# At most two attention steps behind one FFN step from block 2 on, and q of tile 5 loaded ahead of V of tile 4

## Chip, cores and metric

The kernel runs on one core of one Trainium2 chip. The metric is the device time of one execution in microseconds (us): the median of 5 runs of the kernel before is 341.76 us (341.69 to 342.01).

## What is computed

Causal attention with a sliding window of 128 keys and a bias that falls linearly with distance (8 batches, 8 heads, 576 positions, head size 64), and a gated feed-forward block (FFN) on its output, 4608 tokens of 512 wide:

```python
scores = scale * q @ k.T + slopes * (-abs(rel))        # only where 0 <= rel < 128
attn = exp(scores - max) / sum
x = (attn @ v).transpose(0, 2, 1, 3).reshape(4608, 512)
g = x @ w_gate                                         # 512 x 1536
out = (g * sigmoid(g) * (x @ w_val)) @ w_out           # 1536 x 512
```

## The kernel before

**Attention** works on 36 units, nine for each pair of batches (`units`): eight tiles of 128 queries, and one unit that joins the two leftover half tiles. For unit i, `scores(i)` (line 244) takes products of k and q on TensorE (line 280) into four PSUM banks, four exponentials on ScalarE (line 286), and two products with a mask on VectorE (line 292). `weighted(i)` (line 328) multiplies the exponentials with V on TensorE (`av`, line 348) in two halves of four heads, each into a bank of its own, and divides by the sums on VectorE (lines 350 and 351). `x_transposed(i)` brings the result into the layout that the FFN reads (`xT`).

**The FFN** works on nine blocks of 512 tokens. For each of 12 slices of the inner width, `gate_val` (line 432) makes two groups of four matmuls (line 400): `pg` with the gate weights, after which ScalarE makes a tanh (`tt`, line 418) and VectorE a product (`uu`, line 419), and `pv` with the value weights, after which VectorE makes `hT` (line 430). The output products are made for the block before, in between (line 454 for block 0; line 535, with sums of tiles S from lines 488 to 491, for the later ones). Blocks 6 to 8 use another scheme for the first products (line 624), when attention is over.

**PSUM.** The banks of `scores`, of `av` and of some others come from one pool of four buffers in turn (`ps_a`, tag a). A bank is taken again when its reader is done. `pg` and `pv` come from another pool of three (`ps_f`, tag gv).

**The order.** Both parts are generators. `attention()` (line 851) yields after each attention step: the products and the first exponential of `scores` are a step each, the second exponential with the first mask product is one, and so on; from unit 13 on (`LATE`), `weighted(i)` stands inside of `scores(i + 1)`, as a step after the third. `ffn()` yields after each FFN step, with the amount of work (1.0 for a `pg` or a `pv` group, 0.75 for an output product). `everything()` (line 950) takes one FFN step, and then attention steps until their number `n_att` reaches a target that grows with the FFN's work (lines 976 to 984), or until enough tiles are done for the block that comes next (`ready`):

```python
            else:
                target = 84 + (step - 57) * RATE / 34.5
            while (n_att < target or done < ready[blk]) and att_step():
                pass
```

From step 60 on, the last step of block 1, the program's order is binding for TensorE alone (lines 965 to 967). On ScalarE and VectorE a scheduler sets the order when the kernel is built; in the trace each engine starts its instructions in that order.

**Loads.** GpSimd issues the loads of k, q, V and the weights, in an order written out by hand for the first eleven tiles (lines 892 to 925). Each load signals one of eight completion semaphores, in turn, and a load is issued only when the load eight places before it, on the same semaphore, has landed. Tiles 4 to 10 of k and q are transposed on TensorE (line 218), tiles from 11 on by a DMA that SyncE issues (line 239).

Of the kernel before, what the change touches and what calls it, by code (L numbers as in the profile page):

```python
# [51 lines left out]
def kernel(  # L52
# [54 lines left out]
    def later_masks(n, many):  # L107
        for h in by_slot[n:n + many]:
            nc.scalar.activation(reg[:, slot(h), :], dist, AF.Exp, scale=-(2.0 ** (-8.0 * (h + 1) / H)))
# [15 lines left out]
    def make_masks():  # L125
        nc.scalar.copy(msk[0][:, :, 0:64], reg[:, :, 128:192])
        nc.scalar.copy(msk[1][:, :, 64:128], reg[:, :, 128:192])
        nc.scalar.copy(msk[2][0:64, :, 0:64], reg[0:64, :, 0:64])
        nc.scalar.copy(msk[2][64:128, :, 64:128], reg[64:128, :, 64:128])
# [18 lines left out]
    def busy(n):  # L148

        t_ = ps_f.tile([P, 512], FP32, name="nil", tag="po", bufs=1)  # L150
        for _ in range(n):
            nc.tensor.matmul(t_, idle[:, 0:P], idle, start=True, stop=True)
# [20 lines left out]
    def source(src, rank):  # L173

        s, c = divmod(rank, 9)
        if c == 8:
            return [((64 * n, 64 * n + 64),
                     src[2 * s + n, :, 512:576, :].rearrange("h p d -> p h d")) for n in range(2)]
        b, t = 2 * s + c // 4, c % 4
        return [((0, P), src[b, :, t * P:(t + 1) * P, :].rearrange("h p d -> p h d"))]  # L180

    def load_v(rank):
        va[rank] = va_all[rank % NV]
        for (p0, p1), src in source(v, rank):
            nc.gpsimd.dma_start(va[rank][p0:p1, :, 0:D], src)  # L185

    def load_qk(rank, which="kq"):
        for name in which:
            t_ = nat.tile([P, H, D], FP16, name=name + "n", tag=name + "n")
            for (p0, p1), src in source(k if name == "k" else q, rank):  # L190
                nc.gpsimd.dma_start(t_[p0:p1], src)  # L191
            (natk if name == "k" else natq)[rank] = t_

    def load(rank):
        load_qk(rank)
        load_v(rank)
# [626 lines left out]
    def first_tiles():  # L823

        first_masks()
        transposes_to(need[0] + 1)
        for n, _ in enumerate(run(scores(0))):
            if n == 0:
                transposes_to(need[1])
        for i in range(FIRST):  # L830
            if i + 1 < FIRST:
                for n, _ in enumerate(run(scores(i + 1))):
                    if n == 0 and i + 2 < FIRST:
                        transposes_to(need[i + 2])
            weighted(i)

            if i >= 2:
                begin(4, i - 1)
            if i > 0:
                x_transposed(i - 1)  # L840
        begin(6, 2)
        begin(4, 3)
        gate(0, 0, early[(0, 0, "g")][0], 0, 384)
        x_transposed(FIRST - 1)
        val(0, 0, early[(0, 0, "v")][0], 0, 384)
        later_masks(0, 2)
        gate(0, 1, early[(0, 1, "g")][0], 0, 384)
        val(0, 1, early[(0, 1, "v")][0], 0, 384)
        begin(6, 3)
# [35 lines left out]
    def load_w(c0, c1):  # L885
        for src, dst in ((wg2, wg_sb), (wv2, wv_sb)):
            nc.gpsimd.dma_start(dst[:, :, c0:c1], src[:, :, c0:c1])
# [13 lines left out]
    load_w(0, 256)  # L901
    load_w(256, 512)
    load_w(512, 768)
    load(4)
    load_qk(5, "q")
    load_w(768, 1024)
    load_qk(5, "k")
    load_qk(6)
# [18 lines left out]
    done = n_att = 0  # L927
    ready = [4, 8, 13, 17, 22, 26, 31, 35, 36]

    def att_step():  # L930
        nonlocal done, n_att
        r = next(att, None)
        if r is not None:
            done = r
            n_att += 1
        return r is not None
# [7 lines left out]
    def progress(steps):  # L944
        total = 0.0
        for size in steps:
            total += size
            yield total

    def everything():  # L950
        nonlocal done
        base = 0
        busy(WARM)
        with tc.manual_schedule(engines=ENGINES[MANUAL]):
            first_tiles()
            done = FIRST
            steps = progress(ffn())
            while (at := next(steps)) < ALONE:
                if at == 2.0:
                    nc.scalar.copy(idm2, idm)  # L960
                if at in (1.0, 3.0, 4.0):
                    later_masks(2 * (1, 3, 4).index(at) + 2, 2)
        fixed = ExitStack()
        for step in steps:
            if step >= FIXED_FROM and fixed is not None:
                fixed.enter_context(tc.manual_schedule(engines=ENGINES["pe"]))
                fixed, held = None, fixed
            if step == MASKS_AT:
                make_masks()

            b1 = 24 + 3 * PRE

            lead = LEAD if done < X_DMA_FROM - 2 else LEAD + 4
            blk = (0 if step + LEAD < b1 else 1 if step + LEAD < 60
                   else min(NBLK - 1, 2 + int((step + lead - 60) // 34.5)))
            if step < b1:

                target = base + 1.25 * max(0, step - ALONE) + 1.5 * max(0, step - 16)
            elif step < 60:
                target = base + 32 + SECOND * 8 * (step - b1) / (60 - b1)  # L980
            else:
                target = 84 + (step - 57) * RATE / 34.5
            while (n_att < target or done < ready[blk]) and att_step():
                pass
        held.close()

    everything()
    queue.close()

# [29 lines left out]
```

## Time and profile before

| what | value |
|---|---|
| median of 5 runs | 341.76 us (341.69 to 342.01) |
| the profiled execution's own time | 341.76 us |
| its span, first to last instruction | 340.0 us, so 1.76 us lie around it |
| granted TensorE clock, mean | 0.996 |
| busy share of the span: TensorE, VectorE, ScalarE, GpSimd | 97%, 81%, 61%, 32% |
| chain of work that ended last | TensorE 72%, VectorE 18%, ScalarE 5% |

In the views, PE is TensorE's matmuls, PEld its weight loads, DVE VectorE, ACT ScalarE, POOL GpSimd. A row of the timeline gives the start, the length of the merged run of instructions, engine, line, output and inputs, and in brackets the idle time of the engine just before, with what ended it. Matmul ends are modelled and reach past the start of the next one, so lengths of neighbours overlap; the distance between starts is what the engine spends.

### The profile page before, as it was taken

The page shows a single profiled execution, that of the slowest core. Times are in us where ns is not written, and L with a number is a line of the kernel's source. Part 1 is how long each engine was busy: PE and PEld are TensorE (multiplying, and loading weights), DVE is VectorE, ACT ScalarE, POOL GpSimd, SP SyncE. Part 2 cuts the span into 40 slices and gives each one's busy share as a digit, 9 for nine tenths or more (in the row PEclk, how much of TensorE's full clock was granted, in tenths as well). Part 3 has the DMA queues.
Part 4 walks back from the last instruction along what each step waited for, and adds up shares of the span by engine and source line. Part 5 has one row for each costly group of instructions (what it writes and reads, how often), then busy time and mean ns, then how long its engine had stood idle before and what let it go on. Part 6 is the DMA issues. An engine that isn't in the chain of part 4 may idle for free.

```text
span 340.0 us, 7782 instructions
## 1 busy us (share of the span) xinstructions
PE 329.9 (97%) x2983; PEld 219.2 (64%) x2983; DVE 276.6 (81%) x651; ACT 207.3 (61%) x413; POOL 109.6 (32%) x136
## 2 busy tenths in 40 slices
PE   7999999999999999999999999999999999999994
PEld 4484445444455665566665655666688888888883
DVE  5577985999888779998899999999865885775682
ACT  3758676565675676666665647563467776776650
POOL 8968682548765267644008000000000000000000
PEclk9999999999999999999999999999999999999998
DMA  9999999899999999999979903031101101011014
GB/s 150 167 180 177 166 164 161 75 134 153 153 168 155 157 175 176 158 161 146 191 139 104 177 19 94 15 61 49 64 2 62 52 12 65 2 63 64 0 64 124
DMA packets 160037, 37.37 MB, mean 110 GB/s; under 512 B 147328, under 2 KB 155648, under 8 KB 160000
## 3 DMA queue, kind: packets, MB, share of 16 engines
q0 software_dynamic: 118336, 18.62, 82.3%
q1 hardware_dynamic: 40976, 17.64, 28.1%
q10 hardware_dynamic: 688, 0.62, 0.6%
q8 instruction: 23, 0.38, 0.5%
q14 instruction: 14, 0.11, 0.1%
HBM read 37.91 MB, written 9.44 MB: 139 GB/s over the span
## 4 chain that ended last, share of the span: by engine, by line
PE 72%; DVE 18%; ACT 5%; issue 3%; DVEq 0%; ACTq 0%
PE po L535 15%; PE pg L400 12%; PE pv L400 11%; PE gX L624 9%; PE gY L624 5%; DVE hT L430 4%; PE av L348 4%; DVE uu L419 3%; PE ps L280 3%; PE p L535 3%; PE gZ L624 2%; DVE x L351 2%; DVE ex L292 2%; PE po L454 2%; ACT tt L418 2%
## 5 line engine op out<-in xcount | busy, mean ns | idle before, releaser
L400 PE MATMUL pv<-xT,wv_sb 128*128 128x512 f16 (+2 forms) x320 | 76.5, 358 | 0.6 <-DVE uu L419 0.2
L400 PE MATMUL pg<-xT,wg_sb 128*128 128x512 f16 (+2 forms) x320 | 75.8, 358 | 0.3 <-DVE xT L376 0.2
L418 ACT ACTIVATE tt<-pg 128x512 f16<-128x512 f32 (+2 forms) x70 | 41.3, 590 | 47.9 <-PE pg L400 47.0
L286 ACT ACTIVATE ex<-ps 128x512 f16<-128x512 f32 x96 | 50.0, 605 | 10.1 <-PE ps L280 10.1
L419 DVE SCALAR_TENSOR_TENSOR uu<-tt,pg 128x512 f16<-128x512 f16 (+2 forms) x69 | 46.0, 667 | 10.6 <-ACT tt L418 10.5
L430 DVE TENSOR_TENSOR hT<-uu,pv 128x512 f16<-128x512 f16 (+2 forms) x70 | 46.7, 667 | 3.0 <-PE pv L400 1.3
L185 POOL DMA_DIRECT2D va<-in_v_dram x40 | 34.2, 864 | 36.2 <-PE av L348 28.3
L400 PEld LDWEIGHTS <-wv_sb 128*128 128x128 f16 x320 | 28.3, 98 | 25.1 <-issue 3.2
L535 PEld LDWEIGHTS <-hT 128*128 128x128 f16 x384 | 37.2, 98 | 10.7 <-issue 0.8
L400 PEld LDWEIGHTS <-wg_sb 128*128 128x128 f16 x320 | 28.2, 98 | 23.3 <-issue 2.2
L191 POOL DMA_DIRECT2D kn<-in_k_dram x39 | 33.3, 858 | 18.1 <-DMA kT<-kn 11.5
L191 POOL DMA_DIRECT2D qn<-in_q_dram x39 | 33.4, 861 | 17.9 <-DMA va<-in_v_dram 10.8
L535 PEld LDWEIGHTS <-S 128*128 128x128 f16 x288 | 27.4, 98 | 7.2 <-issue 1.4
L292 DVE TENSOR_TENSOR ex<-ex,m_reg 128x1024 f16<-128x1024 f16 x42 | 28.8, 687 | 2.9 <-ACT ex L286 2.8
L351 DVE TENSOR_TENSOR x<-av,rec 128x256 f16<-128x256 f32 x72 | 28.8, 420 | 0.4
L535 PE MATMUL po<-T,S 128*128 128x256 f16 x192 | 25.9, 273 | 0.3 <-ACT u2s L561 0.3
L535 PE MATMUL po<-T,hT 128*128 128x256 f16 x192 | 26.0, 272 | 0.1
L320 ACT ACTIVATE exc<-psc 128x512 f16<-128x512 f32 x40 | 21.3, 607 | 1.9 <-PE psc L316 1.9
L678 DVE TENSOR_TENSOR hT<-s,v 128x512 f16<-128x512 f16 x18 | 7.6, 424 | 17.7 <-ACT s L677 17.7
L348 PEld LDWEIGHTS <-ex 128*128 128x128 f16 x384 | 17.4, 97 | 4.6 <-issue 1.3
L348 PE MATMUL av<-va,ex 128*128 128x65 f16 x384 | 19.3, 193 | 0.7 <-ACT ex L286 0.7
L280 PE MATMUL ps<-qT,kT 64*128 64x256 f16 x192 | 17.1, 272 | 0.4 <-DVE qT L223 0.2
(134 smaller groups left out, 537.7 us busy)
## 6 DMA issues: line engine op xcount, KB each, us to landing
out_dram<-osb SPq DMA_DIRECT2D x32, 256.0 KB, 2.8
va<-in_v_dram POOLq DMA_DIRECT2D x32, 128.0 KB, 8.2
qn<-in_q_dram POOLq DMA_DIRECT2D x31, 128.0 KB, 9.4
kn<-in_k_dram POOLq DMA_DIRECT2D x31, 128.0 KB, 9.8
wg_sb<-in_moe_w_gate_dram POOLq DMA_DIRECT2D x6, 256.0 KB, 7.7
wv_sb<-in_moe_w_val_dram POOLq DMA_DIRECT2D x6, 256.0 KB, 8.3
wo_sb<-in_moe_w_out_dram POOLq DMA_DIRECT2D x2, 768.0 KB, 9.1
kn<-in_k_dram POOLq DMA_DIRECT2D x8, 64.0 KB, 7.0
```

The costliest lines, as they stand in the source:

```text
L185: nc.gpsimd.dma_start(va[rank][p0:p1, :, 0:D], src)
L191: nc.gpsimd.dma_start(t_[p0:p1], src)
L286: nc.scalar.activation(e[:, o:o + 2, :], banks[q4][par], AF.Exp, scale=scale)
L292: nc.vector.tensor_mul(e[:, o, :], e[:, o, :], reg[:, o, :])
L348: nc.tensor.matmul(av[:, j, :], w, val, start=(n == 0), stop=(n == len(todo) - 1))
L351: nc.vector.tensor_mul(x[:, 4 * half:4 * half + 4, :], av[:, :, 0:D], rec.broadcast_to([P, 4, D]))
L400: nc.tensor.matmul(ps[:, c0:c1], w[:, kb, ms], xT[n][:, kb, c0:c1], start=(kb == 0 and c0 == 0), stop=(kb == NKB - 1 and c1 == 512), skip_ ...
L418: nc.scalar.activation(tt, pg[:, c0:c1], AF.Tanh, scale=0.5)
L419: nc.vector.scalar_tensor_tensor(out=uu, in0=tt, scalar=one if (n, m) == PIN else 1.0, in1=pg[:, c0:c1], op0=ALU.add, op1=ALU.mult)
L430: nc.vector.tensor_mul(hT[n][:, m, c0:c1], acted[(n, m)][1][:, c0:c1], pv[:, c0:c1])
L535: nc.tensor.matmul(dst, a[:, m, cols], b[:, m, :], start=(start and m == 0), stop=(m == HM - 1), skip_group_check=True)
L624: nc.tensor.matmul(dst[:, i, :], w[:, kb, c0 + i * P:c0 + (i + 1) * P], a[:, kb, :], start=(start and i == 0 and kb == 0), stop=(i == 1 an ...
```

## The change

```diff
@@ the loads, from line 901
     load_w(0, 256)
     load_w(256, 512)
     load_w(512, 768)
-    load(4)
+    load_qk(4)
     load_qk(5, "q")
+    load_v(4)
     load_w(768, 1024)
     load_qk(5, "k")
     load_qk(6)
@@ everything(), from line 980
                 target = base + 32 + SECOND * 8 * (step - b1) / (60 - b1)
             else:
                 target = 84 + (step - 57) * RATE / 34.5
-            while (n_att < target or done < ready[blk]) and att_step():
+            most = n_att + 2 if step >= 60 else 1000
+            while (n_att < min(target, most) or done < ready[blk]) and att_step():
                 pass
```

`load(4)` is k, q and V of tile 4, in this order. The first part swaps two loads of 128 KB in GpSimd's queue. The second part caps the attention steps that the target asks for behind one FFN step at two, from step 60 on; the steps that `ready` asks for are not capped.

## Prediction

> **What bounds the kernel now.** I read the page first, then busy times stretch by stretch, then the chain of waits and the timeline where the two programs' orders differ.
>
> ```profile
> PE 72%; DVE 18%; ACT 5%; issue 3%; DVEq 0%; ACTq 0%
> ```
>
> ```profile
> 94.00:108.00 14.00, 13.09 (x120) 7.69 (x119) 12.44 (x27) 9.78 (x20) 8.14 (x11) 1.00 2.03 163
> 108.00:199.00 91.00, 90.97 (x850) 55.20 (x848) 82.01 (x193) 54.63 (x112) 36.12 (x44) 1.00 1.70 153
> 199.00:242.00 43.00, 42.95 (x367) 25.86 (x366) 42.92 (x108) 22.77 (x46) 0.00 (x0) 1.00 0.20 47
> 242.00:325.00 83.00, 82.96 (x756) 73.82 (x756) 57.11 (x128) 58.08 (x114) 0.00 (x0) 1.00 0.11 39
> ```
>
> After the length come PE, PEld, DVE, ACT, POOL and the clock. TensorE is full from 108 to 325 us at a clock of 1.00, and VectorE too from 199 to 242. So what TensorE loses before 108 us is lost at the end. The waits of PE from 78 to 340 us are three groups (total, times, longest):
>
> ```profile
> PE av L348 <- ACT ex L286: 0.7, 2, 0.5
> PE po L535 <- ACT u2s L561: 0.3, 1, 0.3
> PE px L374 <- DVE x L351: 0.2, 1, 0.2
> ```
>
> The largest lies where the change acts, in the timeline of PE and of ACT:
>
> ```profile
> 94.14 0.61 PE L280 MATMUL ps<-qT,kT 64*128 64x256 f16 x8
> 95.21 0.29 PE L348 MATMUL av<-va,ex 128*128 128x65 f16 x4 [0.46 <-ACT ex L286]
> 95.70 0.29 PE L348 MATMUL av<-va,ex 128*128 128x65 f16 x4 [0.20 <-ACT ex L286]
> 95.83 1.02 PE L400 MATMUL pg<-xT,wg_sb 128*128 128x512 f16 x4
> 96.69 1.03 PE L400 MATMUL pv<-xT,wv_sb 128*128 128x512 f16 x4
> ```
>
> ```profile
> 94.56 2.06 ACT L286 ACTIVATE ex<-ps 128x512 f16<-128x512 f32 x4 [0.58 <-PE ps L280]
> 96.89 0.60 ACT L418 ACTIVATE tt<-pg 128x512 f16<-128x512 f32 x1 [0.26 <-PE pg L400]
> ```
>
> The products of unit 14 take all four banks of pool a. Each half of `av` of unit 13 needs one of them back, so it stands until the first exponential ends (94.56 + 0.60 = 95.16) and then the second (95.06 + 0.59 = 95.65, single rows). The `pg` behind, four matmuls for bank gv, needs none of that, and starts only when `av` has gone.
>
> **The cap: what moves.** Following `n_att` by hand through `everything()`, 85 steps are done before step 60. There the target, 84 + 3 x 54/34.5 = 88.7, asks for four (to 89); the next FFN steps ask for 2, 1 and 1. Capped, it is 2, 2, 2, 2: the same 93 after four FFN steps. Nowhere later do more than two come. The two programs' orders agree: on PE one place differs, the four `pg` of block 2's first slice stand between the products of unit 14 and the eight `av` of unit 13, not behind them. ACT's and SP's orders are unchanged. On DVE some eight instructions around it change places.
>
> **The cap: TensorE's sum.** After the products the next product of full height can start 0.55 us after their start: at 99.16 the same eight start, and the `pv` behind them at 99.71. So `pg` starts at 94.14 + 0.55 = 94.69 in place of 95.83. Its four take 96.69 - 95.83 = 0.86, to 95.55. Then `av`: the first half (its bank is free since 95.16) takes 4 x 0.032 = 0.13, to 95.68; the second starts at 95.70 as before, behind the second exponential; `pv` starts at 95.83 in place of 96.69. **Gain: 0.86 us**, all of `pg`, laid into two holes of 95.21 - 94.69 = 0.52 and 95.70 - 95.34 = 0.36. Bounds: the two idle times that the view prints, 0.46 + 0.20 = 0.66, and both holes, 0.88. I take 0.86, because the second half of `av` can't start before its exponential.
>
> The Trainium skill's page "TensorE: Matmul & The Clock Gate", section "Back-to-back issue gap", speaks against this size: it gives some 131 ns for a matmul of 512 columns in a sustained stream, where this trace has 0.86/4 = 215 ns. By the page, as an estimate, four would hide 0.52 us and the time would be 341.24 us; the trace decides.
>
> **The cap: does it last to 108 us?** ACT: the exponentials run to 96.49 (94.56 + 4 x 0.48), so `tt` starts there, 0.4 earlier. VectorE's rows before:
>
> ```profile
> 95.95 0.69 DVE L292 TENSOR_TENSOR ex<-ex,m_reg 128x1024 f16<-128x1024 f16 x1
> 96.97 0.67 DVE L292 TENSOR_TENSOR ex<-ex,m_reg 128x1024 f16<-128x1024 f16 x1
> 97.88 0.68 DVE L419 SCALAR_TENSOR_TENSOR uu<-tt,pg 128x512 f16<-128x512 f16 x1
> 100.88 0.69 DVE L292 TENSOR_TENSOR ex<-ex,m_reg 128x1024 f16<-128x1024 f16 x1 [0.29 <-ACT ex L286]
> 101.48 0.68 DVE L430 TENSOR_TENSOR hT<-uu,pv 128x512 f16<-128x512 f16 x1
> 104.68 0.69 DVE L430 TENSOR_TENSOR hT<-uu,pv 128x512 f16<-128x512 f16 x1
> 106.02 0.69 DVE L419 SCALAR_TENSOR_TENSOR uu<-tt,pg 128x512 f16<-128x512 f16 x1 [0.65 <-ACT tt L418]
> ```
>
> By the distance of starts (0.6 for a row of 0.68, 0.33 for one of 0.42, 0.1 for a reciprocal) the new order runs: L489 at 95.54, first mask product 95.85, two reciprocals 96.45, two `x` 96.66, `uu` 97.33 (its `tt` ends at 97.09), second mask product 97.93, `hT` 98.53, L490 99.13, `uu` 99.46 (its `tt` ends at about 99.0, 0.86 earlier), L491 100.06, next mask product 100.39, `hT` 100.99. That is 0.49 earlier than 101.48, and the waits in front of `uu` at 99.90 and of the mask product at 100.88 are gone. So VectorE is only 0.49 early, to 104.68. What TensorE, 0.86 early, takes from VectorE there has more cover than the difference of 0.37. The smallest is the second mask product: moved 0.96 later it ends at 98.6, and the `av` that reads it comes at 101.24 - 0.86 = 100.38: 1.8 us. At 106.02 VectorE has idled 0.65 for a `tt` that follows TensorE, so from there it is 0.86 early too. The 0.3 wait at 107.78 is behind `u2s`, fourth in ACT's queue after that `tt`; it moves along.
>
> **From 108 us to the end** the orders are the same, and what each engine takes comes from engines that are 0.86 early. Only loads could be late. They run ahead of TensorE: GpSimd stands 8.69 us before 121.81 and 19.57 us before 178.06 for an `av` to free a V buffer, and no row of PE's waits above names a DMA. VectorE's full stretch from 199 us begins with an idle time of 0.74 for `tt`, so it starts early as well. I cost the rest at nothing; the price if this cover is gone is the whole 0.86.
>
> **The two loads.**
>
> ```profile
> 16.44 0.89 POOL L185 DMA_DIRECT2D va<-in_v_dram  x1
> 17.32 0.89 POOL L191 DMA_DIRECT2D qn<-in_q_dram  x1
> 26.44 0.54 PEld L218 LDWEIGHTS <-qn 128*128 128x128 f16 x8
> 27.38 0.59 PE L400 MATMUL pv<-xT,wv_sb 128*128 128x512 f16 x2 [0.23 <-DVE uu L419]
> ```
>
> They land 9.6 and 9.4 us after issue, so at about 26.0 and 26.7: q of tile 5 lands just as its four transposes come, the second half of the eight at 26.44. Eight without a wait take 0.098 + 7 x 0.056 = 0.49, so 0.05 was lost. Swapped, q lands 0.6 earlier and the 0.05 goes, but TensorE then waits for `uu` (0.23 at 27.38) that much longer. VectorE copies this tile only at 28.77. V lands at 26.7 and is first read at 38.39: 12 us of cover. The two swap their completion semaphores, and the issues behind them on those (26.43 and 27.17) find landings of the same size in the same places. Gain 0, bounds 0 and 0.05.
>
> The Trainium skill's page "DMA: Bandwidth & Descriptors", section "Two DMAs through the same engine are not ordered", says that nothing orders DMAs across the 16 engines, so that order of issue need not be order of landing. Here the two landed in order, 0.7 apart; by the page the swap could bring nothing, and the sum stays.
>
> **Sum.** Span 340.0 - 0.86 = 339.14; with 1.76 around it 340.90 us. The profiled execution's 341.76 is also the median.
>
> **Rivals.**
> 1. *All of it arrives*: 340.9 us (340.7 to 341.07). For it: TensorE's full stretch behind.
> 2. *VectorE hands on its own 0.49 only*, where one of its results has less cover than I see: 341.76 - 0.49 = 341.27. For it: VectorE is 89% busy from 94 to 108. Against it: 0.65 of idle time at 106.02.
> 3. *It doesn't do what it is for*: the cap acts at one place in the whole program, and a later wait (banks, loads, VectorE's full stretch at 199) takes all of it back: 341.76 us. For it: 0.86 of 340 is one hole. Against it: the idle times of 8.69, 19.57 and 0.74.
> 4. *Slower*, by the second mask product of unit 14. It now stands behind `uu`, thus behind a `tt` that stands behind four exponentials. If it ends after 100.38, the `av` of unit 14 stands, and all behind it; each us beyond costs one. The gain is gone from 101.24, and slower shows from 101.92, 3.3 us later than my 98.6. Four us late, at 102.6, TensorE loses 102.6 - 100.38 = 2.2 and the time is 340.9 + 2.2 = 343.1 us. Against it: `tt` has its input at 95.7 and ACT is free at 96.49.
>
> **Chances.** 0.64, 0.13, 0.14 and 0.09. A change within 0.2% (0.68 us) can't be told from none: faster means under 341.08, which rival 1 alone gives, so faster 0.64, same 0.27, slower 0.09. Range: from 341.76 - 0.88 - 0.05 less the spread of the runs, 0.32, to rival 3 plus 0.25: 340.5 to 342.0; outside lie rival 4 and a little below.
>
> **What would show it.** Right: `pg` at 94.7 with no idle time of `av` before the first half, `pv` at 95.8, `hT` near 101.0, `po` at 106.9 (107.78), gaps after 108 us as now. Wrong: a wait of PE on DVE or a DMA between 96 and 199 that before lacks. For the loads: no missing 0.05 in the eight transposes, and `pv` still at 27.38.

## The result and the profile after

The median after the change is **340.81 us** (22 runs, 340.41 to 341.19), against 341.63 us of the kernel before (42 runs, 341.22 to 342.01): a ratio of 0.9977, interval 0.9971 to 0.9983. That is 0.23% faster, between 0.17% and 0.29%, which is 0.58 to 0.99 us. The prediction called more than 0.2% (0.68 us) faster: the middle of the interval lies above that, its lower end does not. The profiled execution took 340.72 us with a span of 338.9. Among the runs of the experiments below, one of experiment 2 (379.77 us, at a granted clock of 0.85) and one of experiment 4 (1182.75 us) count in the medians and not in the ratios.

The chain of work that ended last, on the page of the kernel after, has more of TensorE and less of VectorE in it (before: 72% and 18%):

```profile
PE 74%; DVE 15%; ACT 5%; issue 2%; DMA 1%; SPq 0%; DVEq 0%; ACTq 0%
```

Busy times by stretch (length, then PE, PEld, DVE, ACT, POOL, and the granted clock), where the change acts and behind it:

```profile
94.00:108.00 14.00, 13.75 (x138) 8.36 (x137) 13.18 (x28) 9.89 (x21) 8.28 (x10) 1.00 2.05 156
108.00:199.00 91.00, 90.97 (x840) 54.86 (x837) 81.99 (x194) 55.25 (x113) 36.45 (x45) 1.00 1.75 155
```

PE is busy for 13.75 of the first 14 us in place of 13.09, which is 0.66 more, the two idle times of 0.46 and 0.20. From 108 to 199 us its busy time is the same to the hundredth. The waits of PE from 78 to 340 us (total, times, longest):

```profile
PE po L535 <- ACT u2s L561: 0.3, 1, 0.3
PE px L374 <- DVE x L351: 0.2, 1, 0.2
```

The group of `av` is gone, the other two are left as they were, and no new one has come. The place itself, in PE's timeline:

```profile
94.16 0.61 PE L280 MATMUL ps<-qT,kT 64*128 64x256 f16 x8
94.70 1.04 PE L400 MATMUL pg<-xT,wg_sb 128*128 128x512 f16 x4
95.58 0.43 PE L348 MATMUL av<-va,ex 128*128 128x65 f16 x8
95.85 1.02 PE L400 MATMUL pv<-xT,wv_sb 128*128 128x512 f16 x4
...
106.94 0.81 PE L535 MATMUL po<-T,S 128*128 128x256 f16 x6 [0.25 <-ACT u2s L561]
```

`pg` now stands ahead of `av`, and no brackets are left on either: while the exponentials free the banks, TensorE does the four matmuls that it did behind `av` before. `pv` starts at 95.85 (96.69). VectorE, in its timeline:

```profile
97.97 0.69 DVE L292 TENSOR_TENSOR ex<-ex,m_reg 128x1024 f16<-128x1024 f16 x1
...
101.04 0.68 DVE L430 TENSOR_TENSOR hT<-uu,pv 128x512 f16<-128x512 f16 x1
...
104.23 0.69 DVE L430 TENSOR_TENSOR hT<-uu,pv 128x512 f16<-128x512 f16 x1
105.18 0.69 DVE L419 SCALAR_TENSOR_TENSOR uu<-tt,pg 128x512 f16<-128x512 f16 x1 [0.26 <-ACT tt L418]
```

The second mask product of unit 14 has moved back from 96.97 to 97.97; the two `hT` come 0.44 and 0.45 earlier (101.48 and 104.68 before), and the `uu` at 106.02 comes 0.84 earlier, after 0.26 us of idle time in place of 0.65.

Laid over each other matmul by matmul, the two traces give the whole account. From 56 to 95 us each matmul of the kernel after starts 0.02 **later** than its counterpart before. From the `pv` at 96.69 (before's time) it starts 0.84 **earlier**, and that distance does not change up to the last matmul, which ends at 334.65 in place of 335.49. So 0.86 us was gained at one place, in one step, and none of it was given back.

### The profile page after: what moved, and what is told of

Same layout as the page of the kernel before. It is cut to its first block, busy times and chain, and to the rows that moved or that the text cites. A ratio compares the mean times of both kernels' runs of the same rounds, so it can differ in the third digit from the quotient of the medians.

```text
span 338.9 us, 7782 instructions
## 1 busy us (share of the span) xinstructions
PE 329.0 (97%) x2983; PEld 218.3 (64%) x2983; DVE 276.5 (82%) x651; ACT 207.2 (61%) x413; POOL 109.6 (32%) x136
## 4 chain that ended last, share of the span: by engine, by line
PE 74%; DVE 15%; ACT 5%; issue 2%; DMA 1%; SPq 0%; DVEq 0%; ACTq 0%
PE po L535 16%; PE pg L400 13%; PE pv L400 12%; PE gX L624 9%; PE gY L624 5%; PE av L348 4%; PE ps L280 4%; DVE hT L430 3%; DVE uu L419 3%; PE p L535 3%; PE po L454 2%; PE gZ L624 2%; PE px L374 2%; ACT tt L418 2%; DVE x L351 1%
```

## The experiments

Each time is a median. Each ratio is to runs of the kernel before on the same chip, with its interval.

**1. The cap alone.** The two loads stay in the order of before.

```diff
-    load_qk(4)
+    load(4)
     load_qk(5, "q")
-    load_v(4)
```

> The cap without the swap of the loads. Theory (the whole gain is one group of four pg matmuls, 0.86 us, laid into the hole in front of av of unit 13): 0.80 to 0.90 us under the kernel before, ratio 0.9975, pg at 94.7 and pv at 95.8 us as with both parts. Rival (the earlier q of tile 5 gives a part, since TensorE was 0.1 us early from 26 to 55 us in the profile of the changed kernel): 0.7 us or less under before.

Measured: 340.84 us against 341.49, ratio 0.9981 (0.9966 to 0.9996). In PE's timeline the place looks as in the kernel after:

```profile
94.72 1.04 PE L400 MATMUL pg<-xT,wg_sb 128*128 128x512 f16 x4
95.59 0.43 PE L348 MATMUL av<-va,ex 128*128 128x65 f16 x8
95.86 1.03 PE L400 MATMUL pv<-xT,wv_sb 128*128 128x512 f16 x4
```

Laid over before, its matmuls are 0.04 late ahead of the place and 0.82 early behind it: 0.86 again, carried whole. By the time alone the gain is 0.65 us (0.14 to 1.16), which does not exclude the rival's 0.7 or less; the trace does, since it gains the whole step without the swap. The cap alone gives the gain.

**2. The load swap alone**, the cap taken out of the kernel after.

```diff
-            most = n_att + 2 if step >= 60 else 1000
-            while (n_att < min(target, most) or done < ready[blk]) and att_step():
+            while (n_att < target or done < ready[blk]) and att_step():
```

> The swap of the loads without the cap. Theory: ratio 1.000 within 0.0005; the eight weight loads of q lose no 0.05 us any more, and what TensorE is early by after that is gone at 55 to 57 us, where the transposes of q of tiles 9 and 10 wait for their loads; the hole in front of av at 94.7 is as before. Rival: 0.1 us or more under before, carried to the end.

Measured: 341.59 us against 341.49, ratio 0.9999 (0.9988 to 1.0010), no difference. The lengths are read from a second profile of the same kernel:

> The swap alone once more, for a profile at full clock, which the first run of it did not leave. Theory: the eight weight loads of k's and q's transposes at 26 us take 0.49 us in place of 0.54, TensorE still waits for uu at 27.3, the two holes in front of av of unit 13 are 0.5 and 0.2 us as before, and from 96 us on TensorE keeps the distance to before that its first loads gave it at 7 us. Rival: the 0.05 us or more is kept to the end, beyond that distance.

Measured: one run of 341.73 us beside one of 341.53. PE's weight loads, and PE behind them:

```profile
26.59 0.49 PEld L218 LDWEIGHTS <-qn 128*128 128x128 f16 x8
```

```profile
26.64 0.61 PE L218 MATMUL pt<-idm,qn 128*128 128x128 f16 x8
27.52 0.81 PE L400 MATMUL pv<-xT,wv_sb 128*128 128x512 f16 x3 [0.27 <-DVE uu L419]
```

The eight transposes take 0.49, where before had 0.54, and the `pv` behind them waits 0.27 for `uu` in place of 0.23. Against before, this trace is 0.14 late ahead of the transposes, 0.10 late in them, and 0.15 late again from the `pv` on: 0.04 us are won and the next wait takes them back. The two holes at `av`, 0.46 and 0.20, are there unchanged. At 55 to 57 us nothing is lost: this trace has no lead that it could lose.

What was expected for the transposes came, and yet it does not show a gain by the swap. The profiles of experiments 1, 3, 4 and 6, which have the loads in the **old** order, give the same 0.49 and the same wait of 0.27:

```profile
26.29 0.49 PEld L218 LDWEIGHTS <-qn 128*128 128x128 f16 x8
```

This is experiment 4, whose transposes come even 0.15 us earlier than those of before. The landings of q of tile 5 in the traces say why. In the profile of before it landed at 26.70 us, just behind the 26.66 at which its first weight load was due (it came at 26.75). In the four others with the old order it landed at 26.14 to 26.34, 0.37 to 0.60 ahead of that weight load. In the four profiles with the swapped order (the kernel after, experiments 5 and 7, and this one) it landed at 25.45 to 25.77, 0.78 to 1.20 ahead. So the swap does bring q earlier, but only the one execution that was profiled before had a wait there to take away, and `pv`, which waits for `uu` right behind, gives that back.

**3. Extra work in the hole.** Is it the hole that pays, or VectorE's new order? The kernel before makes the four `pg` matmuls twice: one more time, for nothing, just ahead of `av` of unit 13, where the change puts them, and then in their old place. The four extra matmuls are work that the kernel doesn't need.

```diff
+    def twice_pg():
+        ps = ps_f.tile([P, 512], FP32, name="pg", tag="gv")
+        for kb in range(NKB):
+            nc.tensor.matmul(ps, wg_sb[:, kb, 0:P], xT[2][:, kb, :], ...)
+        early[(2, 0, "g")] = (ps, 0)
...
                     if n == 2 and late:
+                        if i == 13:
+                            twice_pg()
                         weighted(i)
```

> The order of before, with the four pg matmuls of block 2's first slice made twice: once for nothing between the products of unit 14 and av of unit 13, and once where they stand. Theory: the first four cost nothing, because av waits there for its banks anyway: 341.6 us, ratio 1.000 within 0.0005, av at 95.6 and pv at 96.7. Rival (TensorE's time counts wherever it is spent, and the gain came from the changed order on VectorE): 0.86 us over before, ratio 1.0025.

Measured: 341.63 us against 341.49, ratio 1.000 (0.999 to 1.001). Its PE timeline, line 855 being the extra `pg`:

```profile
94.79 1.04 PE L855 MATMUL pg<-xT,wg_sb 128*128 128x512 f16 x4
95.67 0.44 PE L348 MATMUL av<-va,ex 128*128 128x65 f16 x8
95.94 1.02 PE L400 MATMUL pg<-xT,wg_sb 128*128 128x512 f16 x4
```

Four matmuls more than before, and the second `pg` starts 0.11 behind before's 95.83, with the products of unit 14 themselves 0.11 behind: the extra work was free. VectorE's order was that of the kernel after as far as the second `x` (the two reciprocals together, then both `x`), and this part of it brought nothing. Behind that it was the order of before, with the second mask product ahead of `uu`. So the rest of VectorE's new order was not run by itself; but in the kernel after, no wait of PE behind 96 us names VectorE.

**4. The same extra work behind the hole.** The call stands after `weighted(i)`, all else as in experiment 3; again the four matmuls are made twice.

```diff
                         weighted(i)
+                        if i == 13:
+                            twice_pg()
```

> The same four pg matmuls made twice, both times behind av of unit 13. Theory: 0.86 us over before, ratio 1.0025, since from there on TensorE is full to the end. Rival (a later wait takes up such an amount, so that 0.86 us at this place is not 0.86 us at the end): under 0.5 us over before.

Measured: 342.52 us against 341.49, ratio 1.0024 (1.0013 to 1.0035), which is 0.82 us (0.44 to 1.20; the two medians lie 1.03 apart). PE's timeline:

```profile
95.03 0.29 PE L348 MATMUL av<-va,ex 128*128 128x65 f16 x4 [0.46 <-ACT ex L286]
95.52 0.29 PE L348 MATMUL av<-va,ex 128*128 128x65 f16 x4 [0.20 <-ACT ex L286]
95.65 1.03 PE L855 MATMUL pg<-xT,wg_sb 128*128 128x512 f16 x4
96.51 1.03 PE L400 MATMUL pg<-xT,wg_sb 128*128 128x512 f16 x4
```

Both holes are back, and the four matmuls take 96.51 - 95.65 = 0.86. Laid over before, this trace goes from 0.17 early to 0.69 late at this place, in one step. The same work costs nothing in front of `av` and its full length behind it. That is the gain of the change, measured from the other side.

**5. `av` later still.** If one `pg` in front of `av` fills the hole, then a `pg` and a `pv` fill it too, and nothing else should differ. The cap is one until step 62.

```diff
-            most = n_att + 2 if step >= 60 else 1000
+            most = n_att + (1 if step < 62 else 2) if step >= 60 else 1000
```

> Both parts of the change, and av of unit 13 one FFN step later still: behind pg and pv of block 2's first slice (the cap is one step until step 62). Theory: the hole is already filled but for some 0.02 us, so 340.8 us as with the change, within 0.15. Rival (each FFN step that is put in between hides as much again): another 0.5 to 0.9 us, about 340.1 us.

Measured: 341.17 us against 341.58, ratio 0.9991 (0.9981 to 1.0001): **neither theory's number**. PE's timeline:

```profile
96.91 0.42 PE L348 MATMUL av<-va,ex 128*128 128x65 f16 x8
...
99.65 0.50 PE L280 MATMUL ps<-qT,kT 64*128 64x256 f16 x5
100.42 0.39 PE L280 MATMUL ps<-qT,kT 64*128 64x256 f16 x3 [0.28 <-DVE x L351]
100.75 1.04 PE L400 MATMUL pg<-xT,wg_sb 128*128 128x512 f16 x4
```

`av` has no wait, as foreseen. But the products of unit 15 now stand closer behind it, and the sixth of them waits 0.28 for `x`: the banks of `av` come free only when VectorE has divided by the sums. I had looked at the wait for `ex` in front of `av` and not at who takes the banks of `av` next. From the first of the eight to the `pg` behind them pass 1.10 us, where 0.55 would do. Laid over before, this trace gains the same 0.86 at `av` (0.48 late to 0.38 early) and gives 0.55 back at these products (to 0.17 late): 0.31 is left. By the ratio the gain is 0.31 too, but between -0.03 and 0.65 (the medians lie 0.41 apart), so only the trace shows that something is left. A hole that is filled by moving a bank's user later can open the next one at that bank.

**6. `av` in other banks.** The kernel before, with the two banks of this `av` taken from the pool of `pg` and `pv`. Does `av` wait for the bank, or for something else that the exponential stands for?

```diff
-            pool, tag = (ps_f, "gv") if i < FIRST else (ps_a, "a")
+            pool, tag = (ps_f, "gv") if i < FIRST or i == 13 else (ps_a, "a")
```

> The kernel before, with the two banks of av of unit 13 taken from the pool of pg and pv (three buffers) in place of the pool of the products. Theory (av waits for banks that the exponentials have to read first): av starts right behind the products at 94.7 us; in its stead pg waits for the bank of the pv before it, until its hT ends at 95.5, and pv for the first x, until about 97.0: between 0.3 us under and 0.4 us over before. Rival (av waits for something else that ScalarE makes): av stays at 95.2 us.

Measured: 341.87 us against 341.58, ratio 1.0008 (0.9999 to 1.0017). PE's timeline:

```profile
94.78 0.43 PE L348 MATMUL av<-va,ex 128*128 128x65 f16 x8
95.64 1.02 PE L400 MATMUL pg<-xT,wg_sb 128*128 128x512 f16 x4 [0.43 <-DVE hT L430]
97.04 1.04 PE L400 MATMUL pv<-xT,wv_sb 128*128 128x512 f16 x4 [0.38 <-DVE x L351]
```

With other banks `av` starts straight behind the products, so the bank was its only wait. Now `pg` and `pv` wait for the three banks of their pool, 0.43 and 0.38, and the time is that of before or a little more (laid over before, 0.26 us are lost). Between the banks of these two pools the wait only changes its place; the order of the work is what filled the hole. A further bank was not tried.

**7. The next hole.** The wait of `po` for `u2s` that both kernels have is of the same kind. In the kernel after, the products of the unit that joins two half tiles stand ahead of the first `po`, so three exponentials stand ahead of `u2s` in ScalarE's order. The edit to the kernel after lets no attention step follow one FFN step (69.25), which puts those products behind this `po`.

```diff
+            if step == 69.25:
+                continue
             most = n_att + 2 if step >= 60 else 1000
```

> The changed kernel, and no attention step behind the FFN step at 69.25: the sixteen products of unit 16 go behind the output product that u2s reads, so that ScalarE makes u2s ahead of their exponentials. Theory (the same kind of hole, 0.41 us in front of the output product at 106.94 us, which waits for u2s behind three exponentials): another 0.35 to 0.41 us, about 340.4 us, and that wait is gone. Rival (the products of unit 16 come later by 0.66 us, and what waits for their exponentials takes the gain): 340.8 us or more.

Measured: **340.20 us** (5 runs) against 341.58, ratio 0.9959 (0.9947 to 0.9972), the fastest of all. ScalarE's timeline in the kernel after, then in this run, and this run's waits of PE from 78 to 340 us:

```profile
105.04 1.57 ACT L320 ACTIVATE exc<-psc 128x512 f16<-128x512 f32 x3
106.48 0.41 ACT L561 ACTIVATE u2s<-po 128x256 f32<-128x256 f32 x1
```

```profile
104.91 0.38 ACT L561 ACTIVATE u2s<-po 128x256 f32<-128x256 f32 x1
105.23 2.06 ACT L320 ACTIVATE exc<-psc 128x512 f16<-128x512 f32 x4
```

```profile
PE px L374 <- DVE x L351: 0.2, 1, 0.2
```

`u2s` runs ahead of all four exponentials (at 106.48, behind three of them, in the kernel after), and the group of `po` is gone. Laid over before, the matmuls are 1.13 early ahead of the place and 1.55 behind it: 0.42 more than by the cap. Of the distance of 1.13, 0.27 is there from the first 10 us on and belongs to no edit. By the time, the gain over before is 1.40 us (0.96 to 1.81), which is 0.58 more than the 0.82 of the change. With five runs that can't be told from 0.42; the size is read from the trace.

## Why the prediction was right

The forecast was 340.90 us, the median is 340.81, and the forecast gain of 0.86 stands beside a measured 0.82 (341.63 - 340.81), with an interval of 0.58 to 0.99. Part of the agreement of the totals is luck: the sum started from 341.76, the median of five runs and the profiled execution, where 42 runs give 341.63. From that base it would have said 340.77. The gain and its place in the trace are the better test. By the steps of the prediction:

- **The bound.** That a loss before 108 us is lost at the end was read from PE's full stretch from 108 to 325. It held in full: the distance of 0.84 stays the same over 239 us, and experiment 4 shows the reverse, four matmuls more at 96 us and 0.82 us more at the end.
- **What moves.** One place on PE, the four `pg`, as it was counted; experiment 1 gives the whole step without the loads.
- **The size.** `pg` was put at 94.69, `av` without a wait, `pv` at 95.83; the trace has 94.70, 95.58 and 95.85. The step behind is 0.86, where the printed idle times (0.66) would have been the lower bound: they are what is left after modelled ends, while the filled holes are counted from start to start. That it is not the upper bound, 0.88, has the reason given: the second half of `av` still starts behind its exponential, at 95.72 where that ends at 95.67, the same 0.05 as in before (95.65 and 95.70). Experiment 3 shows that work in the hole is free, experiment 6 that it is the bank.
- **The price of a matmul.** The Trainium skill's page "TensorE: Matmul & The Clock Gate", section "Back-to-back issue gap", gives some 131 ns for a matmul of 512 columns, by which the gain would have been 0.52. In the trace of experiment 4 four such matmuls, one behind the other with nothing waited for, take 0.86 us, 215 ns each. The measurement decides against that figure here. The interval of that run's time alone, 0.44 to 1.20, would not have told the two apart; that of the change itself, 0.58 to 0.99, leaves 0.52 out.
- **VectorE's hand-over.** The new order was worked out to 97.93 for the second mask product, 100.99 for `hT` and 0.49 early to 104.68. The trace has 97.97, 101.04 and 0.44 to 0.45. TensorE, 0.84 early, didn't wait for any of it: the cover was enough. This is where rival 2 (341.27) would have shown, and it fell; its gain of 0.49 lies outside the interval as well.
- **The late mask product**, rival 4 (343.1): it ends at 98.66, and the `av` that reads it starts at 100.40. 1.74 us of cover are left, where 1.8 were worked out.
- **A later wait that takes all of it**, rival 3 (341.76): PE's waits from 108 on are none, as before. Experiment 5 shows that this rival was near: moved one group further, the same `av` gives more than half of it back, at a bank wait that the prediction did not look at.
- **`u2s`.** Its wait was forecast to move along, from 107.78 to 106.9. It did (106.94). The prediction didn't ask whether the wait could go; experiment 7 did.
- **The load swap, where a reading failed.** It was cost at nothing, because `pv` waits for `uu` whatever the transposes do. The cover holds in each trace: whatever is won in the transposes, `pv` waits that much longer (it starts at 27.27 in the kernel after, which is 0.11 early from the first loads on). Rightly read were that q lands just as its transposes come, in that one execution, and that the swap brings it earlier. But the step "so 0.05 was lost" took a detail of one execution for a cost of the order of the loads: in four profiles with the old order q lands 0.37 to 0.60 us ahead, and nothing is lost. The term was nothing either way, so the sum didn't suffer. Whether the swap ever saves anything stays open; by the time it is nothing within 0.12% (0.9988 to 1.0010).

The predicted range (340.5 to 342.0) was far wider upwards than it had to be: it reaches to rival 3 plus 0.25, because rivals 2 and 3 were given 0.27 together. Rival 4 lay outside it.

## What to carry to other kernels

A matmul that waited for a bank held the independent matmuls behind it as well (`pg` stood behind `av` here), so look at what follows the waiting matmul and whether it may stand in front. Count such a hole from start to start and fill it with a piece of about its length; then follow the moved instruction's own banks to their next user, since a piece too much moves the wait there (experiment 5 kept 0.31 of 0.86 us). When one engine is full for the rest of the span, what is gained ahead of that stretch can arrive whole, as the 0.86 us of the cap and the 0.42 of experiment 7 did, and the list of that engine's waits before it says where to look next.

## What was not expected

Profiles differ where TensorE waits for loads, even where the programs are alike, and by nearly as much as this change brings. From the transposes at 7.61 us (before's time) on, which follow the first loads, the kernel after is 0.11 early against before, experiments 5 and 7 are 0.27 early, and experiments 1 and 3 are 0.06 and 0.14 late, though nothing ahead of that place was changed. In PE's timeline of the kernel after this is the place:

```profile
6.06 0.65 PE L211 MATMUL pt<-stage 128*128 128x128 f32 x4 [0.70 <-DMA stage<-in_q_dram]
```

Most profiles keep their distance up to 95 us. Two lose it at 55 to 57 us, where the transposes of the later tiles need their loads: the kernel after goes from 0.11 early to 0.02 late, and experiment 5 from 0.27 early to 0.48 late, 0.75 us, with a wait of 0.50 for q in its trace. This fits the profiled execution of experiment 5, which took 341.92 us while its median is 341.17, but no other execution of it has a trace to compare. Both profiles that lose it have the loads swapped; two others with the swap keep their distance, as all with the old order do, so whether the swap has a part in it is not shown. So two profiles are compared by the distance of matching instructions on either side of the place, and not by their spans. The runs of before spread over 0.8 us (341.22 to 342.01; beside experiments 1 to 4 one took 343.43); whether these two places explain all of that stays open, since only profiled executions show them.
